# A table of planner settings replaced: 640 rows by 652, in a two-layer attention and feed-forward kernel on one core

## The chip, the cores and the metric

One NeuronCore of one Trainium2 chip runs the program. The metric is device time in microseconds (us) of one launch, as the median of several executions; lower is better. Five engines work side by side, each in its own fixed program order: PE (TensorE, matmuls), DVE (VectorE), ACT (ScalarE), POOL (GpSimd) and SP (which issues DMAs here).

## The reference

Two layers of attention and of a gated feed-forward block over 2048 tokens of width 512, with 32 heads of 16 channels. Both layers use the same weights.

```python
B, S, D, H = 1, 2048, 512, 32        # F = 1792
...
qkv = (x @ wqkv).reshape(B, S, 3, H, Dh)
scores = einsum("bhqd,bhkd->bhqk", q, k) * Dh ** -0.5
p = softmax(scores, axis=-1)
return einsum("bhqk,bhkd->bhqd", p, v).reshape(B, S, D) @ wo
...
return (gelu(x @ w_gate) * (x @ w_up)) @ w_down
...
x = x + attention(layernorm(x));  x = x + ffn(layernorm(x))
x = x + attention(layernorm(x));  x = x + ffn(layernorm(x))
```

## The kernel before

**Work.** Attention is cut into units: a block of up to 512 query tokens times a group of four heads. Each unit's scores are computed twice. The first pass (called p1 in the code) has queries on the partitions and 512 keys along a PSUM bank; it serves only to find the maximum of each row. The second pass (p2) has keys on the partitions and queries along the bank; there the exponential is taken, and its result goes as weights into the matmul with the values. A score matmul uses 32 of the 128 rows of the PE, so four of them for four heads can run beside each other.

**Which engine does what.**
- PE: first-pass scores at L2564, second-pass scores at L2442, probabilities times values at L2467 (four matmuls for each tile of 512), all projections and feed-forward matmuls at L1309, transposes at L1438, and filler matmuls on zeros at L2597, whose result nobody reads. The planner puts fillers in where it reckons that PE has been too idle in the last 3.4 us.
- DVE: the row maxima at L2579, over one bank (output 128x1) or two banks at once (128x2).
- ACT: the exponentials at L2414, over one bank (128x512) or two (128x1024), and copies out of PSUM.
- A folded tile: PE forms the difference of two key tiles' scores (L2387, from keys subtracted on POOL at L2144), ACT takes its positive part (L2394), and DVE adds it to the other tile's scores and takes the maximum in one custom instruction (L2574, followed by a read-out of its accumulator). So one DVE instruction covers two tiles.
- POOL: softmax sums, layer norm, the polynomial around the tanh of the gelu (L1856 to L1866), and the gate's product (L2066, L2084) after ACT has copied the up-projection out (L2064, L2082). The same product can be made by DVE alone (L2059, L2076).
- SP: moves of queries and keys into place and the transposes by DMA.

**What sets the order.** The host runs a planner before the launch: the loop at the end of `_build`. It keeps an estimated clock for each engine, and at each step it emits the next first-pass piece, the next second-pass piece, a value matmul, a piece of other work (a projection, a feed-forward matmul) or a filler. What it emits is appended to the engines' streams; on the chip each engine follows its stream strictly, with semaphores between engines. PSUM's eight banks are shared out: banks 0 to 3 take first-pass tiles, 4 to 6 second-pass tiles and other work, 7 the value sums. When the second pass lags behind, the planner can lend bank 3 and work on pairs there (`bmode`, `lend`), and DVE then gets more single banks.

Twenty numbers steer the choices: how long to wait for a pair (`SPC`, `SPLIT`), how far ahead of DVE and ACT to emit (`S1C`, `S2C`), how much other work may delay scores (`OV`, `LIM`), how far the second pass may lag (`LAG`, `LAGT`, `LAGX`), how many tiles to fold (`FL`, `GL`, `FX`), how large the pieces of other work are (`PIECE`, `GP`), and so on. They are taken from the table `PLAN` anew at each stretch, that is, for every 2 steps of first-pass position (a step is two tiles of 512):

```python
now = clk["pe"]
if pos["p1"] >= STRETCH * stretch[0]:
    if stretch[0] in PLAN:
        SPC, SPLIT, S1C, S2C, OV, LIM, NT, P2B, LAG, LAGT, FL, GL, FX, AHD, DUE, DUEM, PIECE, GP, NPV, LAGX = PLAN[stretch[0]]
    stretch[0] += 1
```

A row stays in force until the next one. There are 4096 tiles in each pass, so some 1024 stretches. What is computed is the same for any table; the order, the pairing and the folding differ.

Of the kernel before, what the change touches and what calls it, by code (L numbers as in the profile page):

```python
# [822 lines left out]
def _build(nc, x_in, wqkv, wo, wg, wu, wd, out, layer_blocks=((512, 512, 512, 512), (512, 512, 512, 256, 256)),  # L823
# [16 lines left out]
    with es:  # L840
# [62 lines left out]
        clk = {e: 0.0 for e in ("pe", "act", "dve", "pool", "sp", "dma")}  # L903
# [1924 lines left out]
```

## Time and profile before

| | us |
|---|---|
| median of 3 runs | 2442.04 |
| lowest and highest | 2441.47 and 2442.51 |
| the profiled execution's own time | 2441.87 |
| its span, first to last instruction | 2440.2 |
| PE busy in it | 2380.9 |
| DVE busy in it | 2382.1 |
| ACT busy in it | 2326.3 |
| POOL busy in it | 1351.0 |

The profile shows one execution. "Busy" is the time in which at least one instruction of the engine was running; instructions of one engine overlap at their ends, so a mean duration is longer than what one more instruction adds. A row of groups reads: line, engine, operation, output and input, shapes, count, then busy time and mean duration in nanoseconds, then the idle time just ahead of those instructions and who ended it.

### The profile page before, as it was taken

Reading aid. Unit: us, or ns where it says so; the run is one execution under the profiler, and the core shown is the slowest. Engines: PE = TensorE matmul, PEld = TensorE weight load, DVE = VectorE, ACT = ScalarE, POOL = GpSimd, SP = SyncE. Lnnn points to the kernel's source line nnn. Section 1 sums busy time; section 2 is a strip of 40 time slices with the busy share of each in tenths; the row PEclk is TensorE's granted clock in tenths of the full one; section 3 lists DMA queues with packets and bytes.
Section 4 is the critical chain, followed back from the end, with each engine's and each line's share of the span. In section 5 each row is a group of like instructions: output and inputs, shape, how many; then the busy total and the mean of one; then the engine's idle time right before and its main releaser. Section 6 shows DMA issues by size and latency. Waiting matters only on the chain.

```text
span 2440.2 us, 69860 instructions
## 1 busy us (share of the span) xinstructions
PE 2380.9 (98%) x29929; PEld 1149.2 (47%) x29929; DVE 2382.1 (98%) x3203; ACT 2326.3 (95%) x3275; POOL 1351.0 (55%) x2232
## 2 busy tenths in 40 slices
PE   8999999999999999999999999999999999999999
PEld 3444544444444444444533455554444444444456
DVE  8999999999999999999999999999999999999995
ACT  7999999999999999999976999999999999999997
POOL 5121137967579756977752211278716892278462
PEclk9999999999999999999999999999999999999999
DMA  3110000000000001001010000000000000000000
GB/s 96 49 60 8 4 13 13 2 4 13 15 11 2 6 9 20 3 8 24 17 25 14 4 5 4 11 15 2 5 13 17 8 2 9 15 12 5 13 10 13
DMA packets 69678, 35.25 MB, mean 14 GB/s; under 512 B 51576, under 2 KB 68344, under 8 KB 69368
## 3 DMA queue, kind: packets, MB, share of 16 engines
q1 hardware_dynamic: 69368, 30.80, 5.2%
q8 instruction: 234, 3.83, 0.6%
q14 instruction: 76, 0.62, 0.1%
HBM read 9.70 MB, written 2.10 MB: 5 GB/s over the span
## 4 chain that ended last, share of the span: by engine, by line
PE 44%; DVE 39%; ACT 16%; issue 1%; POOL 0%; DMA 0%; SPq 0%; ACTq 0%; POOLq 0%; DVEq 0%
DVE PM L2579 36%; PE PS L2564 15%; ACT SCR L2414 14%; PE PS L2467 11%; PE PS L1309 10%; PE PS L2442 4%; PE PS L2597 4%; DVE SCR L2574 2%; ACT SCR L1862 0%; PE PS L2387 0%; ACT AO L2082 0%; ACT SCR L2394 0%; ACT HT L1326 0%; ACT SG L1326 0%; DVE AO L2125 0%
## 5 line engine op out<-in xcount | busy, mean ns | idle before, releaser
L2579 DVE TENSOR_REDUCE PM<-PS 128x2 f32<-128x1024 f32 (+1 forms) x2551 | 2190.7, 924 | 24.3 <-PE PS L2564 7.4
L2414 ACT ACTIVATE SCR<-PS 128x1024 bf16<-128x1024 f32 (+1 forms) x2590 | 2021.9, 886 | 51.6 <-PE PS L2442 34.9
L2564 PE MATMUL PS<-KT,QT 32*128 32x512 bf16 x3899 | 1038.6, 384 | 36.4 <-DVE PM L2579 21.5
L2442 PE MATMUL PS<-QT,KT 32*128 32x512 bf16 (+2 forms) x5120 | 934.3, 340 | 2.2 <-ACT SCR L2414 1.0
L2467 PE MATMUL PS<-VP,SCR 128*128 128x51 bf16 (+1 forms) x16384 | 818.0, 187 | 9.1 <-ACT SCR L2414 5.8
L2467 PEld LDWEIGHTS PS<-VP,SCR 128*128 128x128 bf16 x16384 | 581.7, 96 | 500.5 <-issue 414.0
L2564 PEld LDWEIGHTS PS<-KT,QT 32*128 32x128 bf16 x3899 | 247.5, 91 | 505.5 <-DVE PM L2579 303.2
L2597 PE MATMUL PS<-WV,ZER 128*128 128x240 bf16 x1961 | 370.7, 265 | 0.1
L1710 POOL TENSOR_TENSOR RL<-ACCS,CM 128x16 f32<-128x16 f32 (+2 forms) x70 | 181.1, 2587 | 305.8 <-ACT ACCS L1704 305.5
L2442 PEld LDWEIGHTS PS<-QT,KT 32*128 32x128 bf16 x5120 | 242.1, 91 | 55.9 <-ACT SCR L2414 28.6
L1651 POOL TENSOR_TENSOR PM<-PM 128x32 f32<-128x32 f32 (+2 forms) x80 | 19.1, 239 | 351.4 <-DVE PM L2579 341.2
L2597 PEld LDWEIGHTS PS<-WV,ZER 128*128 128x128 bf16 x1961 | 149.3, 96 | 55.6 <-issue 50.6
L1309 PE MATMUL PS<-WD,HT 128*128 128x512 bf16 x448 | 138.9, 381 | 0.2 <-ACT AO L1728 0.2
L1309 PE MATMUL PS<-XNT,WU 128*128 128x512 bf16 (+2 forms) x616 | 138.6, 323 | 0.5 <-ACT SCR L2394 0.3
L1309 PE MATMUL PS<-XNT,WG 128*128 128x512 bf16 (+2 forms) x616 | 137.3, 323 | 0.3 <-DVE XNT L1324 0.3
L2084 POOL TENSOR_TENSOR HT<-HT,AO 128x512 bf16<-128x512 bf16 (+1 forms) x96 | 104.3, 1089 | 45.0 <-ACT AO L2082 43.8
L2574 DVE CUSTOM_DVE_ANT_0 SCR<-PS,SCR 128x512 bf16<-128x512 f32 x197 | 126.1, 684 | 0.6 <-PE PS L2564 0.2
L2144 POOL TENSOR_TENSOR KD<-KT 128x512 bf16<-128x512 bf16 x78 | 89.9, 1152 | 65.9 <-PE PS L2387 60.6
L1856 POOL TENSOR_TENSOR SCR<-HT 128x512 bf16<-128x512 bf16 x98 | 101.8, 1039 | 31.2 <-ACT HT L1326 29.9
L2394 ACT ACTIVATE SCR<-PS 128x1024 bf16<-128x1024 f32 x99 | 104.5, 1056 | 13.7 <-PE PS L2387 8.9
L1866 POOL TENSOR_TENSOR HT<-HT,SCR 128x512 bf16<-128x512 bf16 x98 | 112.8, 1152 | 4.4
L1860 POOL TENSOR_TENSOR SCR<-SCR,HT 128x512 bf16<-128x512 bf16 x98 | 112.7, 1152 | 1.6
(130 smaller groups left out, 1493.5 us busy)
## 6 DMA issues: line engine op xcount, KB each, us to landing
KT<-SG SPq DMA_DIRECT2D x64, 64.0 KB
QT<-SG SPq DMA_DIRECT2D x52, 64.0 KB
QT<-MT SPq DMA_DIRECT2D x200, 1.0 KB
out_dram<-AO SPq DMA_DIRECT2D x16, 128.0 KB, 1.7
WG<-in_B_w_gate_dram SPq DMA_DIRECT2D x4, 448.0 KB, 4.8
WU<-in_B_w_up_dram SPq DMA_DIRECT2D x4, 448.0 KB, 5.2
QT<-MT SPq DMA_DIRECT2D x104, 0.5 KB
WD<-in_B_w_down_dram SPq DMA_DIRECT2D x4, 384.0 KB, 3.9
```

Source lines behind the costliest of these rows:

```text
L1309: ins = e.matmul(out_ap, lhsT=l, rhs=r_, start=(i == 0), stop=(i == n - 1))
L1710: emit("pool", lambda e: e.tensor_tensor(RL[:, s, 0:4 * nq], lsum, CM1[:, 0:4 * nq], op=ALU.pow), r=[("ACCS", s), ("CM1",)], w=[("RL", s)] ...
L1860: emit("pool", lambda e: e.tensor_tensor(u, u, ht, op=ALU.mult), r=ku + kh, w=ku, dur=0.18 + n / 520.0)
L1866: emit("pool", lambda e: e.tensor_tensor(ht, ht, u, op=ALU.mult), r=ku + kh, w=kh, dur=0.18 + n / 520.0)
L2394: emit("act", lambda e: e.activation(PT[:, s0:s0 + cnt, :], PS[:, bk:bk + cnt, :], ACTF.Relu), r=bks, w=[("PT", s0 + d) for d in range(cnt ...
L2414: emit("act", lambda e: e.activation(dst, src, ACTF.Exp, scale=DH ** -0.5), r=[BK[bk + i] for i in range(cnt)], w=[("PT", i) for i in slot ...
L2442: ins = e.matmul(bank(bk)[:, i * n:(i + 1) * n], lhsT=KT[32 * j:32 * j + 32, g, kt * 128:(kt + 1) * 128], rhs=QT[32 * j:32 * j + 32, s, c0 ...
L2467: ins = e.matmul(acc, lhsT=PT[:, slot, i * nh + (qt - q0) * 128:i * nh + (qt - q0 + 1) * 128], rhs=AP(VP, (kt * H + 4 * g + j) * 17, [[NTT ...
L2564: ins = e.matmul(bank(b), lhsT=QT[32 * j:32 * j + 32, s, qt * 128:(qt + 1) * 128], rhs=KT[32 * j:32 * j + 32, g, kb * 512:(kb + 1) * 512], ...
L2574: emit("dve", lambda e, i=i, b=b, sl=sl: e.tensor_tensor_reduce(PT[:, sl, :], bank(b), PT[:, sl, :], 1.0, -3.0e38, ALU.add, ALU.max, po[:, ...
L2579: emit("dve", lambda e: e.tensor_reduce(po, PS[:, bs[0]:bs[0] + cnt, :], axis=AX.X, op=ALU.max), r=bks, w=[("PM", sm) + h[1:] for h in hs] ...
L2597: return e.matmul(PS[:, b, NACC:512], lhsT=ZER[:, :], rhs=WV[:, 0, 0:512 - NACC], start=(b != 7), stop=(b != 7), skip_group_check=True)
```

## The change

`PLAN` is replaced: 652 rows in place of 640, and only 14 of them are as they were. The planner gets two further options, `PB` (when POOL is due, the planner gives it the most urgent chain) and `SLF` (layer norm on another path); both have the default 0, and nothing sets them, so the branches are not entered. The rest of the kernel is as it was; lines below the table stand 12 to 19 lines lower.

```diff
 PLAN = {
-    0: (0.3, 0.25, 0.55, 0.42, 0.0, -0.05, 1, 1, 62, 92, 8, 20, 0.5, 1.5, -10, 18, 1, 3, 7, 92),
-    1: (0.3, 0.05, 0.55, 0.42, 0.0, -0.05, 1, 1, 62, 0, 8, 20, 0.5, 1.5, -10, 18, 1, 3, 7, 92),
+    0: (0.3, 0.25, 0.55, 0.42, 0.0, -0.05, 1, 1, 62, 92, 8, 20, 0.5, 1.5, -5, 18, 1, 3, 7, 8),
+    1: (0.3, 0.25, 0.8, 0.42, 0.0, 0.0, 1, 1, 62, 92, 3, 80, 0.5, 1.5, -5, 18, 2, 1, 7, 30),
...
-           ... XDN=2, PK=1, LT=0, RCD=0):
+           ... XDN=2, PK=1, LT=0, RCD=0, PB=0, SLF=0):
...
-            ln = ln_fast if fast else ln_pool if LNP and ...
+            ln = ln_fast if fast or (SLF and LT and tts[0] >= SLF and ((tag[0] == "mid") == (tag[1] == 0))) else ln_pool if LNP and ...
...
-                            if est(a[1], a[2]) > now + 0.3:
+                            if (PB and a[0] == "pool") or est(a[1], a[2]) > now + 0.3:
                                 break
...
+                if PB and clk["pool"] <= now + PB + 1e-6:
+                    ready = [c for c in chains if not c.done and c.ann[0] == "pool" and est(c.ann[1], c.ann[2]) <= now + 0.3]
+                    if ready:
+                        min(ready, key=lambda c: c.due).step()
+                        changed = True
...
+                    if PB and a[0] == "pool":
+                        nxt.append(clk["pool"] - PB)
```

The new table moves nearly every instruction of every engine, but the counts change little. Counted over the whole streams (lines as before the change):

| engine, instruction | before | changed |
|---|---|---|
| DVE L2579 maximum over one bank | 1400 | 1392 |
| DVE L2579 maximum over two banks | 1151 | 1152 |
| DVE L2574 folded tile | 197 | 200 |
| DVE L1324 copy to SG, 512 wide | 5 | 6 |
| DVE L2059 gate product, 512 wide | 5 | 2 |
| DVE L2076 gate product, 512 wide | 2 | 3 |
| ACT L2414 exponential over two banks | 1506 | 1459 |
| ACT L2414 exponential over one bank | 1084 | 1178 |
| ACT L2394 positive part, two banks / one | 98 / 1 | 99 / 2 |
| ACT L2082 / L2064 copy, 512 wide | 82 / 9 | 81 / 12 |
| ACT L1326 copy to SG, 512 wide | 51 | 50 |
| PE L2564 first-pass score tiles | 3899 | 3896 |
| PE L2597 fillers | 1961 | 1866 |
| PE changes between score matmuls (32 rows) and full matmuls (128 rows) | 5374 | 5426 |

Of the exponentials of the first 2048 second-pass tiles (the first layer), 544 were over one bank and 752 over two; now 642 and 703. In the second layer it was 541 and 754, now 537 and 756.

The first place is ACT in the first layer, from the copy-out that ends the 26th unit (L1704, now L1716). L2414 is the exponential, L1326 and L2082 are copies out of PSUM, L1862 a tanh. Before:

```order
L1704 ACTIVATE ACCS<-PS 128x272
L2414 ACTIVATE SCR<-PS 128x512
L1326 ACTIVATE SG<-PS 128x256
L2414 ACTIVATE SCR<-PS 128x1024
L2414 ACTIVATE SCR<-PS 128x512
L2414 ACTIVATE SCR<-PS 128x1024
L2414 ACTIVATE SCR<-PS 128x512
L1326 ACTIVATE HT<-PS 128x512
L2414 ACTIVATE SCR<-PS 128x1024
```

The same place on ACT in the changed kernel:

```order
L1716 ACTIVATE ACCS<-PS 128x272
L2426 ACTIVATE SCR<-PS 128x512 x3
L1338 ACTIVATE HT<-PS 128x512
L2426 ACTIVATE SCR<-PS 128x512 x7
L1874 ACTIVATE SCR<-SCR 128x512
L2426 ACTIVATE SCR<-PS 128x512 x2
L1338 ACTIVATE HT<-PS 128x512
L2426 ACTIVATE SCR<-PS 128x512 x5
```

Exponentials that stood in turn over two banks and over one now come over one bank each: the unit that follows has 60 single and 2 double ones, where it had 22 and 21.

The second place is the end of the first pass on PE. L2564 (now L2576) is the last first-pass score tile; L2442 are second-pass scores, eight matmuls of 128 columns for two tiles, L2467 value matmuls, L1309 with WD the feed-forward's down projection. Before:

```order
L2564 MATMUL PS<-KT,QT 128x512
L2467 MATMUL PS<-VP,SCR 128x3x17 x4
L1309 MATMUL PS<-WD,HT 128x512 x2
L2442 MATMUL PS<-QT,KT 128x128 x16
L2467 MATMUL PS<-VP,SCR 128x51 x4
L2467 MATMUL PS<-VP,SCR 128x3x17 x4
L1309 MATMUL PS<-WD,HT 128x512 x5
L2442 MATMUL PS<-QT,KT 128x128 x8
```

The same place on PE in the changed kernel:

```order
L2576 MATMUL PS<-KT,QT 128x512
L2454 MATMUL PS<-QT,KT 128x128 x8
L2479 MATMUL PS<-VP,SCR 128x3x17 x12
L2479 MATMUL PS<-VP,SCR 128x51 x4
L2454 MATMUL PS<-QT,KT 128x128 x8
L1321 MATMUL PS<-WD,HT 128x512 x2
L2454 MATMUL PS<-QT,KT 128x128 x8
```

From there to the end the streams are nearly alike. Behind the last first-pass tile stand 160 second-pass matmuls of 128 columns (40 tiles) where there were 168 (42 tiles), and 45 down-projection matmuls where there were 51.

More of the change, by code (lines that the diff above doesn't have):

```diff
@@ L823, in _build @@
 def _build(nc, x_in, wqkv, wo, wg, wu, wd, out, layer_blocks=((512, 512, 512, 512), (512, 512, 512, 256, 256)),
-           n_ahead=6, n_pre=6, S1C=0.45, S2C=0.42, OV=0.3, PD=80, FDUE=20, LIM=-0.05, NT=1, AHD=2.0, DUEM=2, FDL2=0, OPD=12, URG=0.3, ft_tok=512, n_pt=8, n_qt=8, SPLIT=0.15, SPC=0.1, PVC=47, WARM=0.55, WARML=0.42, NPV=7, BOOST=0.0, LAG=62, LAGT=84, GP=2, SING=0, DUE=0, END=360, LAGE=10, FD=205, FDL=-10, QD=60, KD_=16, VD=20, FL=8, FMAX=6, NKD=2, FLOOK=2, FX=0.3, GF=0, FAST=1, TG=1, GS=2, P2B=1, PIECE=2, GL=60, GLE=20, HARD=-1e9, LNP=1, LNPT=12, PREO=1, SPL=2, OPL=1, BM=1, LAGB=60, PREO0=1, LNPT0=8, LNPT1=8, QH0=2, QH1=2, OPS=12, FDS=0, FD3=205, FDA=0, SPL0=4, VCH=0, TA=0, TC=0, X3=0, TH=0, HQ=0, TP=1, LAGX=84, G2=0, CAL=0, XD=15, XDT=0.6, XDN=2, PK=1, LT=0, RCD=0):
+           n_ahead=6, n_pre=6, S1C=0.45, S2C=0.42, OV=0.3, PD=80, FDUE=20, LIM=-0.05, NT=1, AHD=2.0, DUEM=2, FDL2=0, OPD=12, URG=0.3, ft_tok=512, n_pt=8, n_qt=8, SPLIT=0.15, SPC=0.1, PVC=47, WARM=0.55, WARML=0.42, NPV=7, BOOST=0.0, LAG=62, LAGT=84, GP=2, SING=0, DUE=0, END=360, LAGE=10, FD=205, FDL=-10, QD=60, KD_=16, VD=20, FL=8, FMAX=6, NKD=2, FLOOK=2, FX=0.3, GF=0, FAST=1, TG=1, GS=2, P2B=1, PIECE=2, GL=60, GLE=20, HARD=-1e9, LNP=1, LNPT=12, PREO=1, SPL=2, OPL=1, BM=1, LAGB=60, PREO0=1, LNPT0=8, LNPT1=8, QH0=2, QH1=2, OPS=12, FDS=0, FD3=205, FDA=0, SPL0=4, VCH=0, TA=0, TC=0, X3=0, TH=0, HQ=0, TP=1, LAGX=84, G2=0, CAL=0, XD=15, XDT=0.6, XDN=2, PK=1, LT=0, RCD=0, PB=0, SLF=0):
     S = x_in.shape[1]
@@ L1467, in ln_to_xnt @@
         def ln_to_xnt(tts, tag, ready, due, fast=False):
-            ln = ln_fast if fast else ln_pool if LNP and tts[-1] < (LNPT if tag[0] == "in" else (LNPT0, LNPT1)[tag[1]]) else ln_head
+            ln = ln_fast if fast or (SLF and LT and tts[0] >= SLF and ((tag[0] == "mid") == (tag[1] == 0))) else ln_pool if LNP and tts[-1] < (LNPT if tag[0] == "in" else (LNPT0, LNPT1)[tag[1]]) else ln_head
             if LT:
```

1260 rows, old and new, of the table PLAN are left out of this document.

## The prediction

> **What bounds the kernel now.** I read the page first, for busy shares and the granted clock:
>
> ```profile
> span 2440.2 us, 69860 instructions
> PE 2380.9 (98%) x29929; PEld 1149.2 (47%) x29929; DVE 2382.1 (98%) x3203; ACT 2326.3 (95%) x3275; POOL 1351.0 (55%) x2232
> ...
> DVE  8999999999999999999999999999999999999995
> ACT  7999999999999999999976999999999999999997
> ...
> PEclk9999999999999999999999999999999999999999
> ...
> PE 44%; DVE 39%; ACT 16%; issue 1%; POOL 0%; DMA 0%; SPq 0%; ACTq 0%; POOLq 0%; DVEq 0%
> ...
> L2579 DVE TENSOR_REDUCE PM<-PS 128x2 f32<-128x1024 f32 (+1 forms) x2551 | 2190.7, 924 | 24.3 <-PE PS L2564 7.4
> ```
>
> Three engines are nearly full, and the chain of waits passes among PE, DVE and ACT. DVE is idle least. Its row maxima alone (L2579) take 2190.7 us. The view by windows, cut at the layer crossing and the tail, shows where DVE is not full (the third figure behind the length is DVE, the fourth ACT):
>
> ```profile
> core 0: us, PE busy (x) PEld busy (x) DVE busy (x) ACT busy (x) POOL busy (x), PEclk, DMA share, GB/s
> 0.00:61.00 61.00, 54.74 (x362) 24.23 (x363) 54.61 (x115) 45.65 (x68) 35.79 (x72) 0.97 0.32 96
> 61.00:671.00 610.00, 594.95 (x7595) 287.81 (x7594) 607.59 (x827) 602.78 (x788) 288.30 (x519) 1.00 0.07 18
> 671.00:1220.00 549.00, 540.04 (x6743) 253.23 (x6744) 545.50 (x687) 537.25 (x800) 411.91 (x665) 1.00 0.06 11
> 1220.00:1342.00 122.00, 117.25 (x868) 47.39 (x867) 119.00 (x221) 82.54 (x119) 48.27 (x113) 1.00 0.09 20
> 1342.00:1830.00 488.00, 479.27 (x6415) 237.62 (x6415) 481.35 (x611) 481.97 (x593) 201.78 (x305) 1.00 0.03 7
> 1830.00:2379.00 549.00, 536.82 (x7024) 259.66 (x7021) 541.13 (x674) 532.14 (x832) 351.13 (x532) 1.00 0.04 10
> 2379.00:2440.00 61.00, 57.79 (x935) 39.22 (x933) 32.97 (x74) 44.02 (x81) 13.87 (x28) 1.00 0.05 13
> ```
>
> From 61 to 2379 us DVE is idle for 2.41 + 3.50 + 3.00 + 6.65 + 7.87 = 23.4 us of 2318. So the time is: DVE's work up to the last row maximum, its idle time on the way, and a tail behind it. The waits of DVE say who makes the idle time:
>
> ```profile
> DVE AO L2125 <- PE PS L1309: 15.3, 4, 8.8
> DVE PM L2579 <- PE PS L2564: 7.4, 18, 1.2
> DVE PM L2579 <- PE PS L2442: 7.2, 33, 0.6
> ```
>
> L2125 belongs to the tail. In the body DVE waits for PE, 14.6 us, because PE has other work queued ahead of the next score tile. The rest of the idle time are gaps too short to be listed.
>
> **The change part by part.** The settings compute nothing; they decide order, pairing, folding and filling. So I cost the counts first, then what order alone can do.
>
> *DVE's work.* The groups by shape:
>
> ```profile
> L2414 ACT ACTIVATE SCR<-PS 128x1024 bf16<-128x1024 f32 x1506 | 1457.0, 1076 | 37.2 <-PE PS L2442 25.8 <-DVE PM L2574 0.4 <-PE PS L2564 0.2
> L2579 DVE TENSOR_REDUCE PM<-PS 128x2 f32<-128x1024 f32 x1151 | 1398.4, 1218 | 17.0 <-PE PS L2442 5.1 <-PE PS L2564 5.0 <-PE PS L2387 0.3
> L2579 DVE TENSOR_REDUCE PM<-PS 128x1 f32<-128x512 f32 x1400 | 938.8, 682 | 7.3 <-PE PS L2564 2.4 <-PE PS L2442 2.1
> L2414 ACT ACTIVATE SCR<-PS 128x512 bf16<-128x512 f32 x1084 | 616.1, 622 | 14.4 <-PE PS L2442 9.0
> L2574 DVE CUSTOM_DVE_ANT_0 SCR<-PS,SCR 128x512 bf16<-128x512 f32 x197 | 126.1, 684 | 0.6 <-PE PS L2564 0.2 <-PE PS L2442 0.2
> L2574 DVE DVE_READ_ACCUMULATOR2_ANT PM<- 128x1 f32 x197 | 16.4, 83 | 0.0
> L2059 DVE TENSOR_TENSOR HT<-PS,HT 128x512 bf16<-128x512 f32 x5 | 3.4, 684 | 0.0
> ```
>
> Neighbours overlap, so the means (1218 and 682 ns) are too long for what one more costs. A second bank adds 1218 - 682 = 536 ns. With the page's 2190.7 us for all 2551, a single one adds (2190.7 - 1151 x 0.536) / 2551 = 0.617 us and a double one 1.153. The changed streams have 8 singles fewer, -4.9 us, and 1 double more, +1.2. Three folded tiles more cost 3 x (0.64 + 0.08) = +2.2 at most (126.1 / 197, and the read-out 16.4 / 197). One copy more to SG is +0.6 (512 wide from PSUM, as L2059, less the same 65 ns of overlap), three L2059 fewer -1.9, one L2076 more +0.6. Sum: **-2.2 us**.
>
> The three gate products that leave DVE go to ACT (L2064) and POOL (L2066). POOL is busy for 55% and hides them; without that cover each would cost ACT about one single exponential.
>
> *ACT's work.* 47 double exponentials become 94 single ones; the first layer alone gives up 49, the second gains 2. At the means, one split costs 2 x 622 - 1076 = 168 ns, together +7.9 us. At what one more adds (2021.9 us for all 2590 from the page's L2414 row below, second bank 454 ns, so 0.517 and 0.971) it is 63 ns, together +2.9 us.
>
> ```profile
> L2414 ACT ACTIVATE SCR<-PS 128x1024 bf16<-128x1024 f32 (+1 forms) x2590 | 2021.9, 886 | 51.6 <-PE PS L2442 34.9
> ...
> 1403.00:1647.00 244.00, 239.65 (x3363) 124.31 (x3360) 241.23 (x304) 243.98 (x272) 81.05 (x154) 1.00 0.04 9
> 61.00:1220.00 1159.00, 1134.99 (x14337) 541.04 (x14336) 1153.09 (x1513) 1140.03 (x1587) 700.20 (x1184) 1.00 0.06 15
> ```
>
> From 61 to 1220 us, the first layer's attention, ACT is idle for 1159 - 1140.03 = 19.0 us, DVE for 5.9. I cost the splits at **0**, hidden behind DVE; if that cover is gone they cost 3 to 8 us (a rival below). Only in the second layer, 1403 to 1647 us, does ACT stand still for just 0.02 us. That is a run of double exponentials with which the second pass catches up, 358 in a row; the changed stream has 361, and it begins 32 first-pass tiles earlier and covers 540 in place of 539. Three doubles more are 2.9 us there and 2.9 us fewer elsewhere. I count it as moved, 0.
>
> *The tail.* After the last row maximum ACT runs on through double exponentials nearly without a gap, then PE does the last gate, up and down projections:
>
> ```profile
> 2391.96 5.43 DVE L2579 TENSOR_REDUCE PM<-PS 128x2 f32<-128x1024 f32 x6
> ...
> 2397.32 6.52 ACT L2414 ACTIVATE SCR<-PS 128x1024 bf16<-128x1024 f32 x7 [0.64 <-PE PS L2442]
> 2403.72 0.24 ACT L1704 ACTIVATE ACCS<-PS 128x68 f32<-128x68 f32 x1
> 2403.83 7.58 ACT L2414 ACTIVATE SCR<-PS 128x1024 bf16<-128x1024 f32 x8
> ```
>
> The last maximum ends at 2391.96 + 5.43 = 2397.4, so the tail is 42.8 us. Two tiles fewer stand in it, one double exponential: 6.52 / 7 = 0.93, so **-0.9 us**. The six down-projection matmuls fewer lie between exponentials, beside ACT, and count 0. Everything from the last exponential on is the same instruction for instruction.
>
> *DVE's idle time on the way.* Three pieces of the chain in the tail give prices for PE's work:
>
> ```profile
> 2402.71 0.31 PE PS L2467 x8
> 2404.67 0.62 PE PS L2467 x20
> 2415.10 0.41 PE PS L2597 x4
> ```
>
> The idle time is what order alone can change, and no row gives it, so I bound it. If all of the body ran as the first part does (2.41 us idle in 610, 0.395%), 2318 us would hold 9.2 us, a gain of 14.3. If all ran as the last part does (7.87 in 549, 1.43%), it would hold 33.2, a loss of 9.8. Two counts say which end is nearer. One is PE's fillers, put in where the planner found PE waiting: 95 fewer, at 0.41 / 4 = 0.10 us each, -9.7 us. Against that stand 52 more changes between score and full matmuls, 26 more runs. A run of value matmuls costs (0.62 - 0.31) / 12 = 0.026 us for each and 0.31 - 8 x 0.026 = 0.10 once, so +2.7 us. PE is asked for 7.0 us less in all. The other count is of places where more than 1.1 us of other PE work (at such prices) stands between two first-pass steps: about 95 before, about 90 now; at 14.6 us for all, -0.8 us. Between -0.8 and -7.0 I take **-3.0 us**, on the side of the first part.
>
> A rule of the Trainium skill speaks against leaving fillers out: "TensorE: Matmul & The Clock Gate", Part 1, says that after an idle window of about 3.4 us the PE clock falls to half. Before the change the trace shows 1.00 in every window behind 61 us, so no run here shows that rule at work in the body. By the rule the sum would be that of the last rival.
>
> **Sum.** -2.2 - 0.9 - 3.0 = -6.1 us, with splits, moved catch-up and POOL at 0. The profiled execution took 2441.87 us (1.67 more than its span, which I keep). It lies 0.17 under the median of 2442.04. So 2441.87 - 6.1 = **2435.8 us**.
>
> **The rivals.**
>
> *Only moved.* The counts hold, but DVE's idle time stays as it is: what one stretch gains another gives back. For it speaks that DVE's work is the same to 0.1%, and that 14.6 us of listed waits are spread over 51 places. Against it, the 95 fillers. Time 2441.87 - 2.2 - 0.9 = 2438.8.
>
> *ACT becomes the bound in the first layer (the other side).* Each engine keeps its order, so where ACT is late PE stands before the next second-pass matmul, and DVE behind it. Place: units such as the one shown, with 60 single exponentials and 2 double ones where it had 22 and 21. Price: 49 splits in the first layer at 168 ns, 8.2 us, with nothing hidden. It decides from the point where ACT's idle time there, 19.0 us in 1159, isn't at the units with the singles. For it speaks that DVE keeps only 5.9 us of its own idle time there to absorb a late PE. Against it, that ACT has three times as much as DVE. Time 2441.87 - 2.2 - 0.9 + 8.2 = 2447.0, slower.
>
> *A clock lapse.* Fewer fillers let the granted clock fall. In the first window the clock reads 0.97, some 61 x 0.03 = 1.8 us lost; four such lapses in the body would cost 7.3 us against the forecast: 2443.1, and more would pass the old time by over 0.2%. Against it, a clock of 1.00 in every later row, and fillers still 1866.
>
> That the change doesn't do what it says I give no chance: the streams differ everywhere, and the two new options are off.
>
> **How the numbers follow.** A measurement of this kernel can tell about 0.2%, 4.9 us, from no change: 2437.2 and 2446.9 are the marks. Forecast 0.48 (2435.8, its own range 2428 to 2437), only moved 0.34 (within), ACT 0.13 (slower), clock 0.05 (0.02 within, 0.03 slower). So faster 0.48, same 0.36, slower 0.16. The full gain of idle time would give 2441.87 - 3.1 - 14.3 = 2424.5 and the full loss 2448.6. The range leaves a tenth out at each end: 2428 to 2446.
>
> **What would show it.** DVE busy about 2380 us, with 1392 single and 1152 double maxima at 682 and 1218 ns. DVE idle from 61 us to 61 us before the end about 20 us in place of 23.4; under 16 or over 30 says that order did more than I gave it. A tail of about 42 us behind the last maximum. ACT over the first layer with idle time left, some 12 to 16 us in place of 19.0; if it stands at under 5, ACT was the bound. A granted clock of 1.00 in every window. The prediction is wrong if DVE's waits for PE grow, above all in the first layer, where they were smallest.

## The result, and the profile after

| | before | changed | difference |
|---|---|---|---|
| median of 7 runs each, us | 2441.68 | 2433.83 | -7.85 |
| lowest and highest, us | 2441.26 to 2442.51 | 2433.37 to 2434.70 | |
| span of the profiled execution, us | 2440.2 | 2432.1 | -8.1 |
| ratio of the times | | 0.9968 | 95% interval 0.9957 to 0.9980 |

The changed kernel is faster, by a little more than the 6.1 us forecast, and inside the range. The page of the changed kernel, in the order in which the prediction read the old one:

```profile
span 2432.1 us, 69441 instructions
PE 2339.3 (96%) x29581; PEld 1144.6 (47%) x29834; DVE 2375.5 (98%) x3201; ACT 2326.5 (96%) x3325; POOL 1356.5 (56%) x2236
...
PEclk9999999999999999999999999999999999999999
...
DVE 36%; ACT 31%; PE 29%; POOL 2%; issue 1%; DMA 0%; SPq 0%; POOLq 0%; ACTq 0%; DVEq 0%
...
L2591 DVE TENSOR_REDUCE PM<-PS 128x1 f32<-128x512 f32 (+1 forms) x2544 | 2184.3, 923 | 24.3 <-PE PS L2454 8.8
```

PE's figure is not to be compared: 29581 matmuls stand against 29834 weight loads, so some 250 matmul records are missing from this trace. So the drop of 41.6 us in PE's busy time, and its fall in the chain from 44% to 29%, can't be read as a gain: part of them is the 95 fillers fewer, part missing records. DVE is busy for 6.6 us less, nearly all of it in the row maxima (2190.7 to 2184.3). ACT is busy for as long as before, although it has 47 exponentials more.

The view by windows, with the columns of the prediction's table (length; PE, PEld, DVE, ACT, POOL; clock):

```profile
61.00:671.00 610.00, 587.09 (x7520) 287.15 (x7565) 607.10 (x830) 603.67 (x803) 290.34 (x525) 1.00 0.07 18
671.00:1220.00 549.00, 529.91 (x6685) 255.04 (x6757) 545.04 (x697) 539.37 (x835) 412.11 (x663) 1.00 0.06 11
1220.00:1342.00 122.00, 116.48 (x863) 46.67 (x867) 120.03 (x219) 82.36 (x117) 47.66 (x111) 1.00 0.09 20
1342.00:1830.00 488.00, 472.28 (x6386) 236.56 (x6427) 480.75 (x605) 485.05 (x621) 203.89 (x306) 1.00 0.03 7
1830.00:2371.00 541.00, 522.77 (x6862) 254.81 (x6926) 533.88 (x666) 525.60 (x805) 354.13 (x534) 1.00 0.05 10
```

DVE's idle time from 61 us to 61 us before the end is 2.90 + 3.96 + 1.97 + 7.25 + 7.12 = 23.2 us; it was 23.4. By the view of waits the two listed waits of the maxima for PE sum to 14.3 us; they were 14.6:

```profile
DVE PM L2591 <- PE PS L2454: 8.8, 38, 0.7
DVE PM L2591 <- PE PS L2576: 5.5, 13, 1.2
```

So 8 us went, and the idle time on which the prediction put 3 of them is where it was. Most of the 8 went from time that the profile calls busy. Behind a maximum over one bank the next maximum begins 598 ns after that one's start, and behind one over two banks 1132 ns; these are the medians of the start-to-start times in both traces, taken here as the spacing where nothing is waited for. Yet the groups by shape give longer means of one:

```profile
L2591 DVE TENSOR_REDUCE PM<-PS 128x2 f32<-128x1024 f32 x1152 | 1397.2, 1216 | 17.0 <-PE PS L2454 6.1 <-PE PS L2576 4.2 <-PE PS L2399 0.3
L2591 DVE TENSOR_REDUCE PM<-PS 128x1 f32<-128x512 f32 x1392 | 930.6, 680 | 7.3 <-PE PS L2454 2.7 <-PE PS L2576 1.3
```

680 - 598 and 1216 - 1132 are some 82 to 84 ns. An instruction that begins up to that much late still begins before the last one has ended. It loses time, and the engine never shows as idle. Among pairs of neighbouring maxima, the mean spacing behind one over a single bank was 638 ns before and is 635 now; behind one over two banks it is 1137 in both. The late ones are the single banks, and they are a little less late.

With those spacings the time up to the last maximum can be split into work (each maximum at its median spacing, a folded tile at 607 + 60 ns, any other instruction at its duration less 85 ns) and lateness (all the rest, idle or not). Each stage ends with the DVE instruction that completes a given number of the 4096 first-pass tiles (256, 2048, 2560, 3584, 4096), the same in both kernels. The last column says how much sooner the changed kernel gets there:

```
first-pass tiles      work before  now      diff   lateness before  now   diff   end of stage
first 1/16 (fill)       148.5     148.4     -0.1        9.0         8.1   -0.9       -1.0
2nd to 8th             1000.0     999.8     -0.2       15.5        15.8   +0.3       -0.9
9th, 10th (crossing)    270.8     270.8      0.0        6.7         4.7   -2.1       -3.0
11th to 14th            607.6     606.3     -1.3       20.7        18.5   -2.1       -6.4
15th, 16th              306.9     305.9     -1.0       10.7        11.7   +1.0       -6.4
```

Over all (from the unrounded figures) the work fell by 2.5 us and the lateness by 3.8. The first layer (the first eight sixteenths) gave nothing beyond its fill, and the last two sixteenths gave nothing either; the gain is made at the crossing of the layers and in the 11th to 14th sixteenth. Behind the last maximum stands the tail. First DVE's last run of maxima, then ACT, by the timeline of the changed kernel (start, length, what, count; a row that joins several shapes names one, and the nine exponentials at 2387.97 are two over one bank and seven over two):

```profile
2385.62 5.41 DVE L2591 TENSOR_REDUCE PM<-PS 128x2 f32<-128x1024 f32 x6 [0.23 <-PE PS L2454]
...
2387.97 7.82 ACT L2426 ACTIVATE SCR<-PS 128x512 bf16<-128x512 f32 x9
2395.67 0.23 ACT L1716 ACTIVATE ACCS<-PS 128x68 f32<-128x68 f32 x1
2395.78 7.58 ACT L2426 ACTIVATE SCR<-PS 128x1024 bf16<-128x1024 f32 x8
...
2403.35 5.62 ACT L2426 ACTIVATE SCR<-PS 128x1024 bf16<-128x1024 f32 x6
```

The last maximum ends at 2385.62 + 5.41 = 2391.0, where it was 2397.4: -6.4. From there to the end it is 41.1 us, where it was 42.8: -1.7. From the copy-out at 2395.67 (before: 2403.72) to the end the two agree, at 36.4 us. So the tail's gain lies between the last maximum and that copy, 4.6 us where it was 6.3: seven exponentials over two banks began there before, five begin there now (from 2391.08 us on, some 0.92 apart).

**At the crossing** one can see what became less late. ACT's timeline before, in the first unit of the second layer:

```profile
1333.74 1.94 ACT L2414 ACTIVATE SCR<-PS 128x1024 bf16<-128x1024 f32 x2 [0.56 <-PE PS L2442]
1336.24 2.00 ACT L2414 ACTIVATE SCR<-PS 128x1024 bf16<-128x1024 f32 x3 [0.56 <-PE PS L2442]
1338.56 3.87 ACT L2414 ACTIVATE SCR<-PS 128x1024 bf16<-128x1024 f32 x5 [0.32 <-PE PS L2442]
...
1357.95 0.39 ACT L1704 ACTIVATE ACCS<-PS 128x272 f32<-128x272 f32 x1
```

And after:

```profile
1323.99 29.77 ACT L2426 ACTIVATE SCR<-PS 128x1024 bf16<-128x1024 f32 x32 [1.03 <-PE PS L2454]
1353.58 0.47 ACT L1716 ACTIVATE ACCS<-PS 128x272 f32<-128x272 f32 x1
```

Before, the exponentials of this unit come in runs of one to seven, with waits of some 0.2 to 0.6 us for second-pass scores between them; now 32 run without a gap. ACT's waits from 1320 to 1360 us (in total, times, longest), before and then after, of which the longest is each time the one ahead of the unit's first exponential:

```profile
ACT SCR L2414 <- PE PS L2442: 11.6, 14, 6.2
```

```profile
ACT SCR L2426 <- PE PS L2454: 6.3, 2, 5.3
```

From 1320 to 1360 us ACT is busy for 17.96 + 16.02 = 33.98 us before and 19.82 + 18.00 = 37.82 us now, by the view of windows, before and then after:

```profile
1320.00:1342.00 22.00, 21.53 (x299) 11.01 (x295) 21.65 (x31) 17.96 (x21) 2.98 (x12) 1.00 0.02 3
1342.00:1360.00 18.00, 17.26 (x252) 8.83 (x251) 17.54 (x27) 16.02 (x18) 4.73 (x14) 1.00 0.01 3
```

```profile
1320.00:1342.00 22.00, 21.14 (x318) 10.88 (x316) 21.80 (x31) 19.82 (x22) 3.28 (x14) 1.00 0.02 3
1342.00:1360.00 18.00, 17.41 (x273) 9.38 (x272) 17.71 (x26) 18.00 (x21) 6.53 (x14) 1.00 0.01 2
```

The copies of the value sums out of PSUM (L1704, now L1716) mark the same place of the program in both, and show how the second pass gains a lead, if not steadily: -1.4 us at the last unit of the first layer (1222.27 to 1220.88), -4.4 at the first unit of the second (1357.95 to 1353.58), between -1.3 and -6.6 from there to 2086 us, -6.3 at the unit that ended at 2134.73, and -8.1 at the end.

### The profile page after: what moved, and what is told of

It reads as the page before. It is cut to its first block, busy times and chain, and to the rows that moved or that the text cites. A ratio compares the mean times of both kernels' runs of the same rounds, so it can differ in the third digit from the quotient of the medians.

```text
span 2432.1 us, 69441 instructions
## 1 busy us (share of the span) xinstructions
PE 2339.3 (96%) x29581; PEld 1144.6 (47%) x29834; DVE 2375.5 (98%) x3201; ACT 2326.5 (96%) x3325; POOL 1356.5 (56%) x2236
## 4 chain that ended last, share of the span: by engine, by line
DVE 36%; ACT 31%; PE 29%; POOL 2%; issue 1%; DMA 0%; SPq 0%; POOLq 0%; ACTq 0%; DVEq 0%
DVE PM L2591 33%; ACT SCR L2426 28%; PE PS L2576 10%; PE PS L1321 8%; PE PS L2479 6%; PE PS L2454 3%; PE PS L2609 2%; DVE SCR L2586 2%; ACT SCR L2406 1%; ACT SCR L1874 1%; PE PS L2399 0%; ACT HT L1338 0%; ACT AO L2094 0%; POOL HT L1878 0%; ACT ACCS L1716 0%
## 5 line engine op out<-in xcount | busy, mean ns | idle before, releaser
L2591 DVE TENSOR_REDUCE PM<-PS 128x1 f32<-128x512 f32 (+1 forms) x2544 | 2184.3, 923 | 24.3 <-PE PS L2454 8.8
L2426 ACT ACTIVATE SCR<-PS 128x512 bf16<-128x512 f32 (+1 forms) x2637 | 2020.4, 878 | 39.2 <-PE PS L2454 24.8
L2576 PE MATMUL PS<-KT,QT 32*128 32x512 bf16 x3896 | 1039.3, 384 | 50.7 <-DVE PM L2591 24.6
L2576 PEld LDWEIGHTS PS<-KT,QT 32*128 32x128 bf16 x3896 | 247.5, 91 | 500.2 <-DVE PM L2591 307.0
L2609 PE MATMUL PS<-WV,ZER 128*128 128x240 bf16 x1866 | 350.9, 265 | 1.1 <-ACT SCR L2426 0.5
L2609 PEld LDWEIGHTS PS<-WV,ZER 128*128 128x128 bf16 x1866 | 141.9, 96 | 47.0 <-issue 40.7
L1321 PE MATMUL PS<-XNT,WG 128*128 128x512 bf16 (+2 forms) x562 | 121.1, 317 | 5.3 <-issue 3.2
L1321 PE MATMUL PS<-XNT,WU 128*128 128x512 bf16 (+2 forms) x552 | 121.6, 316 | 3.8 <-issue 2.9
L1321 PE MATMUL PS<-WD,HT 128*128 128x512 bf16 x380 | 119.3, 381 | 4.2 <-issue 2.4
L2406 ACT ACTIVATE SCR<-PS 128x1024 bf16<-128x1024 f32 (+1 forms) x101 | 105.8, 1049 | 15.5 <-PE PS L2399 11.3
```

What stands on the lines that cost most here:

```text
L1321: ins = e.matmul(out_ap, lhsT=l, rhs=r_, start=(i == 0), stop=(i == n - 1))
L2406: emit("act", lambda e: e.activation(PT[:, s0:s0 + cnt, :], PS[:, bk:bk + cnt, :], ACTF.Relu), r=bks, w=[("PT", s0 + d) for d in range(cnt ...
L2426: emit("act", lambda e: e.activation(dst, src, ACTF.Exp, scale=DH ** -0.5), r=[BK[bk + i] for i in range(cnt)], w=[("PT", i) for i in slot ...
L2576: ins = e.matmul(bank(b), lhsT=QT[32 * j:32 * j + 32, s, qt * 128:(qt + 1) * 128], rhs=KT[32 * j:32 * j + 32, g, kb * 512:(kb + 1) * 512], ...
L2591: emit("dve", lambda e: e.tensor_reduce(po, PS[:, bs[0]:bs[0] + cnt, :], axis=AX.X, op=ALU.max), r=bks, w=[("PM", sm) + h[1:] for h in hs] ...
L2609: return e.matmul(PS[:, b, NACC:512], lhsT=ZER[:, :], rhs=WV[:, 0, 0:512 - NACC], start=(b != 7), stop=(b != 7), skip_group_check=True)
```

## The experiments

All are timed against the kernel before, side by side on the same chip. "Share" means: us measured, divided by the us that were added to one engine at the prices of the prediction. It is given with the interval that follows from the ratio's.

**Which half of the table does it.** Rows below 512 steer the first layer's first pass, rows from 512 on the second's. First the new rows below 512 with the old ones behind:

```diff
 PLAN = {
-    0: ... 511: (rows before)
+    0: ... 511: (rows of the change)
     512: ... (rows before)
```

> The kernel before, with the new table's rows up to stretch 511 (the first layer's share) and its own old rows from 512 on. If the two halves of a table are worth something by themselves, this takes the first half's part of the change: the first-pass position of the layer crossing came at 1190.0 us before and 1190.7 us after, so +0.7 us, ratio 1.000. If the rows only fit the state that they were chosen in, the old rows meet another state here and do worse: this stream has 1470 single and 1124 double maxima and 189 folded tiles, which at 0.617, 1.153 and 0.72 us is +6.3 us of DVE work against before, ratio about 1.003 or more.

Measured: 2486.46 us, ratio 1.0181 (1.0167 to 1.0195), 45 us slower than before. (The 1190.0 and 1190.7 us of the expectation are where half of the tiles outside folds are done, which is not the same tile in both; the 2048th tile was done at 1174.0 us before and 1173.1 after the change.) Then the other way round, the old rows below 512 and the new ones from there:

```diff
 PLAN = {
     0: ... 511: (rows before)
-    512: ... (rows before)
+    512: ... (rows of the change)
```

> The kernel before, with its own old rows up to stretch 511 and the new table's rows from 512 on. If the halves are worth something by themselves, this holds nearly the whole gain, since the two traces stand level at the crossing and differ by 8 us at the end: about -8 us, ratio 0.9965. If rows only fit their own state, the stream's counts decide: 1414 single and 1152 double maxima, 189 folded tiles, +4.0 us of DVE work, ratio about 1.002 or more.

Measured: 2487.32 us, ratio 1.0184 (1.0169 to 1.0200). Each half worsens when the other is exchanged, so the gain can't be divided between them. The windows of the two mixtures, first the one with the new first half, show where it begins to go wrong:

```profile
1220.00:1342.00 122.00, 116.83 (x775) 45.41 (x785) 116.98 (x217) 74.64 (x117) 48.32 (x109) 1.00 0.10 24
1342.00:1830.00 488.00, 474.98 (x6177) 236.40 (x6213) 475.79 (x615) 469.51 (x591) 202.23 (x300) 1.00 0.03 6
```

```profile
1220.00:1342.00 122.00, 116.06 (x752) 45.91 (x759) 117.27 (x210) 71.81 (x108) 46.48 (x99) 1.00 0.10 22
1342.00:1830.00 488.00, 471.14 (x6273) 236.13 (x6315) 469.05 (x596) 478.09 (x607) 204.92 (x312) 1.00 0.03 7
```

DVE is idle for 5.0 and 4.7 us in the crossing, where the matched tables leave 3.0 and 2.0, and for 12.2 and 19.0 us behind it, where they leave 6.7 and 7.3. By the split into work and lateness, the traced run of the first mixture has 11.6 us more work than before, 27 more lateness (24 of it from the crossing to the 14th sixteenth) and a tail longer by 6.0; the second, by a trace that took 2.5 us more than its median, has 2.0, 33 and 12.6. So the loss is mostly lateness and not a matter of counts. In both mixtures the rows fit badly to a state that other rows left.

**Does a row of the wrong state carry anything at all?** The changed kernel with its own rows below 512 and its row 0 from there on, and then with row 0 alone:

```diff
 PLAN = {
     0: ... 511: (rows of the change)
-    512: ... (rows of the change)
+    512: (row 0 of the change)
```

> The changed kernel with its own rows up to stretch 511 and one row for all the rest, row 0 of its table: settings that were never chosen for the second layer. The old rows put there (1.0181 of before) cost some 44 us against before and 52 against the changed kernel. If a row chosen in another state still carries something of the second layer's needs, one row for all of it does clearly worse than that, ratio 1.025 or more. If it carries nothing, the two are alike, ratio 1.018 within 0.3%.

```diff
 PLAN = {
     0: (row 0 of the change)
-    1: ... (all other rows)
```

> The changed kernel with row 0 of its table as the only row, in force for the whole program. If the choice of rows is worth as much in the first layer as in the second, the loss against the changed kernel is about twice that of one row for the second layer alone. If the second layer alone depends on it, the two are alike. Counted: 1350 single and 1295 double maxima and 78 folded tiles, so by counts alone (0.617, 1.153, 0.72 us) 51 us more DVE work than before.

Measured: 2507.61 us, ratio 1.0266 (1.0248 to 1.0285), and 2549.18, ratio 1.0432 (1.0414 to 1.0451). Foreign rows for the second layer (1.0181) beat this single row there (1.0266), so they still carry something; no other single row was tried. Row 0 for the second layer costs 73.8 us against the changed kernel (2507.61 less 2433.83), and row 0 in the first layer too costs another 41.6. So the choice of rows counts in both layers, and less in the first. Against some 115 us between one row and all 652 (2549.18 less 2433.83), the 7.85 from the old table to the new are a small step.

**What DVE's work is worth.** The term of -2.2 us took DVE's time at its full price. Here maxima over two banks are issued as two over one, with the planner's clocks moved on as for one, so that the order stays as it is. First every 11th, 104 in all:

```diff
+ if cnt == 2 and n_max[0] % 11 == 0:
+     for i, b in enumerate(bs):
+         sch.op("dve", lambda e, i=i, b=b: e.tensor_reduce(po[:, i:i + 1], bank(b), axis=AX.X, op=ALU.max), ...)
+     clk["dve"] = start + 0.066 + cnt * 0.5317
```

> The kernel before, with every 11th maximum over two banks (104 of 1151) issued as two over one bank each, 208 singles more; the planner reckons as if nothing had changed, so the order on PE and ACT is the same. If DVE's work sets the body and one more instruction costs what the groups give (2 x 0.617 - 1.153 = 0.081 us), it takes 104 x 0.081 = +8.4 us, ratio 1.0034. If PE or ACT set the pace, DVE's 23 us of idle time take it in: 0 to +2 us.

Measured: 2443.92 us, ratio 1.0010 (1.0001 to 1.0019), +2.0 us. One split adds 2 x 0.617 - 1.153 = 0.081 us, 104 of them 8.4: a share of 0.24 (0.03 to 0.55). By the split into work and lateness the trace has 6.4 us more work and 4.4 less lateness. Then every 4th, 287 in all (% 4 in the same place):

> The kernel before with every 4th double maximum issued as two single ones (287 of 1151). 104 such splits cost +2.0 us in place of 8.4. If DVE has some 60 us of slack and takes more work in at a steady share, 287 cost 287 / 104 x 2.0 = +5.7 us. If the slack is used up place by place, the share rises: between 5.7 and 287 x 0.081 = +23.2 us.

Measured: 2448.63 us, ratio 1.0026 (1.0016 to 1.0036), +6.2 of 23.2 us: a share of 0.26 (0.17 to 0.38). The share is no higher at the larger load, though DVE is then the larger part of the chain of waits (39% before):

```profile
DVE 52%; PE 36%; ACT 10%; POOL 1%; issue 1%; POOLq 0%; ACTq 0%; DVEq 0%
```

The share has a second reading. In these kernels each of the two maxima waits for its own bank alone and releases it when it is done, where the maximum over two waits for both and holds both. So these shares are what a split costs, with that help in it, and not surely what DVE's time alone costs; the runs don't part the two. The same holds for the exponentials below. The base matters too: at the median spacings a split adds 2 x 598 - 1132 = 64 ns and not 81, and both shares become about a third.

**What a split exponential costs.** Every 8th exponential over two banks in the first layer is issued as two, 94 in all, the order kept in the same way:

```diff
+ if cnt == 2 and units[u][0] == 0 and n_exp[0] % 8 == 0:
+     for i in range(2):
+         sch.op("act", lambda e, i=i: e.activation(PT[:, slots[i], :], bank(bk + i), ACTF.Exp, scale=DH ** -0.5), ...)
+     clk["act"] = start + sw + 0.055 + cnt * 0.4267
```

> The kernel before, with every 8th double exponential of the first layer (94 of 752) issued as two single ones; the planner reckons as if nothing had changed. The change has 49 such splits in the first layer, so this is about twice its dose. If ACT's idle time there (19 us in 1159) hides them: within 1.5 us of before, ratio 1.000. If ACT is the bound at those places: 94 x 0.063 = +5.9 us at what one more adds, up to 94 x 0.168 = +15.8 us at the means, ratio 1.0024 to 1.0065.

Measured: 2444.77 us, ratio 1.0012 (1.0003 to 1.0021), +2.9 of 94 x 0.063 = 5.9 us: a share of 0.49 (0.12 to 0.87). Not hidden, then, though ACT has 19.0 us of idle time there. The same for every third of units 37 to 46, 106 in all, in the run where ACT never stands still:

```diff
+ if cnt == 2 and 37 <= u <= 46 and n_exp[0] % 3 == 0:
```

> The kernel before with every 3rd double exponential of the units 37 to 46 issued as two single ones (106 splits; the second layer's run of doubles, in which ACT stood still for 0.02 us of 244). If ACT is the bound there, as that row says: 106 x 0.063 = +6.7 us at what one more adds, up to +17.8 us at the means. If the pace there is DVE's or PE's: like the 94 splits of the first layer, about +3 us.

Measured: 2447.75 us, ratio 1.0026 (1.0017 to 1.0035), +5.3 of 6.7 us: a share of 0.79 (0.62 to 1.28). By its window ACT is busy for all of 244 us, and DVE has 5.1 us of idle time where it had 2.8:

```profile
1403.00:1647.00 244.00, 240.87 (x3303) 124.18 (x3300) 238.87 (x298) 244.00 (x352) 81.32 (x154) 1.00 0.04 8
```

This fits ACT as the bound there, or nearly; the interval doesn't rule out less.

**Are 95 fillers fewer a cause?** They were the reason for the size of the idle-time term. The kernel before without every 20th filler, 98 of 1961, with the planner reckoning them as if they were there:

```diff
+ n_fill[0] += 1
+ if n_fill[0] % 20 == 0:
+     sch.op = lambda *a, **k: None
  ... (the filler matmul)
+ sch.__dict__.pop("op", None)
```

> The kernel before, with every 20th filler matmul left out (98 of 1961; they compute nothing that is read), all else in the same order. If fillers hold up score matmuls, 98 fewer are worth up to 98 x 0.10 = -9.8 us, and the change's gain would be theirs. If fillers only stand where PE waits anyway, as my stall term took most of them to do, 0 to -2 us, ratio 0.999 to 1.000.

Measured: 2442.48 beside 2442.09 us, ratio 1.0006 (0.9997 to 1.0015): no gain. The interval leaves room for 0.7 us of gain at most (the lowest runs differ by as much, 2440.78 beside 2441.45), where 98 at 0.10 us are 9.8. So nearly all of these 98 stand where PE waits anyway. They are spread evenly; that the 95 of the change are alike wasn't tried. Then the opposite, 96 extra filler matmuls right ahead of first-pass score tiles, one for every 28 steps:

```diff
+ n_p1[0] += 1
+ if n_p1[0] % 28 == 0:
+     n_p1[1] += 1
+ if n_p1[1] and est(w=[BK[7]]) <= clk["pe"] - 0.1:
+     sch.op("pe", lambda e: e.matmul(PS[:, 7, NACC:512], lhsT=ZER[:, :], ...))
```

> The kernel before with 96 more filler matmuls, each put straight ahead of a first-pass score tile (every 28th step), where PE has work to do; the planner doesn't know of them, so the rest of the order is the same. If PE sets the pace of the body, each costs its 0.10 us, and 0.10 more where it breaks up a run of score matmuls: +9.6 to +19 us, ratio 1.004 to 1.008. If DVE sets it, as my sum took it, PE's delay is taken in by the banks ahead of DVE: 0 to +3 us.

Measured: 2445.48 us, ratio 1.0015 (1.0006 to 1.0024), +3.0 of 9.6 us: a share of 0.31 (0.15 to 0.61). So the same matmul costs next to nothing where the planner put it and counts for about a third of its length ahead of a score tile.

**What the fillers are for.** The changed kernel without its 1866 fillers (they multiply zeros, and nothing else is left out), the planner reckoning them as if they were there:

```diff
+ if True:
+     sch.op = lambda *a, **k: None
```

> The changed kernel without any filler matmul (1866 left out; they compute nothing that is read), all else in the same order. If fillers are what keeps PE's clock at full rate, the granted clock falls well under 1.00 and the time rises, by tens of us or more. If the clock stays without them, PE is asked for 187 us less (1866 x 0.10) and DVE's waits for PE shrink: the clock at 1.00 and a time some 0 to 20 us under the changed kernel's.

Measured: 2656.07 us, ratio 1.0863 (1.0826 to 1.0901). Its page, and its window from 61 to 671 us:

```profile
PE 2535.3 (95%) x27716; PEld 1154.1 (43%) x27968; DVE 2420.3 (91%) x3201; ACT 2394.4 (90%) x3325; POOL 1356.6 (51%) x2236
...
PEclk8855556898559976998898655579886688689889
```

```profile
61.00:671.00 610.00, 582.71 (x6138) 256.55 (x6184) 556.46 (x750) 558.11 (x724) 257.20 (x462) 0.70 0.06 16
```

The granted clock falls to 0.70 in that window and 0.77 over the run. So the fillers hold the clock up, and 95 fewer were still enough: the changed kernel's clock is 1.00 in every window shown above.

## Why the prediction was right, and where its steps were not

**Direction and size** held: -6.1 us forecast, -7.85 measured. As an account of where the time went, the sum held too: -2.5 of DVE's work (-2.2 forecast), -3.8 of lateness (-3.0, forecast as idle time) and -1.7 of tail (-0.9) make -8.0, which is the span's change but for rounding. What the single steps were worth as causes is another matter.

**DVE's work, -2.2.** By the split of DVE's time it fell by 2.5, so the prices and the counts were right. What the runs speak against is the step from work to time, "-2.2" taken at full price: splits that added DVE work cost 0.24 and 0.26 of its length (0.03 to 0.55 and 0.17 to 0.38), and in the first of them lateness shrank by 4.4 us of the 6.4 added. Taken the other way, which no run did, 2.2 us less work are worth about 0.6.

**ACT's splits, 0.** "Hidden behind DVE" doesn't stand: the 94 splits of the first layer were not hidden. At their share of 0.49 (0.12 to 0.87) the 49 splits of the first layer, 49 x 0.063 = 3.1 us, cost about 1.5. ACT's idle time there did shrink as foretold, from 19.0 to 1159 - 603.67 - 539.37 = 16.0 us (12 to 16 were forecast); but 19 us of idle time in 1159 aren't a cover for every place. The rival in which ACT becomes the bound of the first layer fell: it asked for +8.2, and the first layer ended 1.4 us earlier. In the very unit that it named, with 60 single exponentials and 2 double ones, the time from copy to copy went from 39.2 to 39.9 us; in another, with 55 and 4 where there were 21 and 22, it went from 39.2 down to 37.4.

**The catch-up run, 0.** ACT stands still for 0.13 us of the 244 from 1403 to 1647 us, as before (0.02). The run was moved, not relieved: it now lasts from 1321.0 to 1659.7 us, where it lasted from 1340.5 to 1679.1.

**The tail, -0.9.** The mechanism held, its size was off: -1.7. Counted was one double exponential fewer, from PE's order behind its last first-pass tile; two are gone, seven to five, since ACT also has one more of them done by the time of the last maximum. 2 x 0.92 is 1.8.

**DVE's idle time, -3.0.** This is the step that was read wrongly. The idle time stayed at 23.2 against 23.4 (about 20 was forecast), and the waits for PE at 14.3 against 14.6 (some 2 of either lie in the first 61 us, which the prediction's "body" leaves out). The prediction named a growth of these waits in the first layer as a sign of being wrong: from 61 to 1220 us the two waits listed above went from 1.7 to 2.6 us, and DVE's idle time from 5.9 to 6.9. It is small, and the crossing and what follows made up for it, but it is the opposite of what the term asked for. The lateness fell by 3.8 all the same, inside what counts as busy. Nor is the reason for its size borne out as a cause: taking 98 other fillers out gained 0.7 us at most.

**What order alone was worth.** With the shares as prices, the span's -8.1 us less the tail (-1.7), less DVE's work (-0.6), less the splits (+1.5) leaves about -7.3 for the order alone, where the prediction took -3.0 between bounds of -14.3 and +9.8. That is worked out, not measured: the shares have wide intervals, come from work added to the kernel before, and the change removes some. By this reckoning two errors stood against each other, on the one side a full price for DVE's work and none for ACT's splits, on the other too little for the order, and that the sum came out better than its terms is luck.

**The other rivals.** "Only moved" (2438.8) asked for unchanged idle time, and got it, but not its time: the gain doesn't show as idle time. The clock lapse didn't come; the clock is 1.00 behind 61 us.

**What is shown and what isn't.** Shown by the traces: at the crossing ACT's short waits for second-pass scores went and DVE's lateness fell by 2.1 us; in the 11th to 14th sixteenth the lateness fell by another 2.1 and DVE's work by 1.3; the tail is shorter by 1.7. Shown by the runs: each half of the new table, put together with the other half of the old one, is 1.8% slower than the old table and 2.2% slower than the new one. Not shown: that ACT's smoother run at the crossing is what made DVE less late there. Not isolated: which rows make the lateness fall behind the crossing, since a mixture of rows changes all that follows it, by 45 us here.

## What to carry to other kernels

Where three engines pass the chain of waits between them, one us of work more on one of them need not be one us more of time: here it was 0.24 to 0.26 on DVE, 0.31 on PE and 0.49 on ACT (0.79 where ACT never rests), each with a wide interval, and a few splits with the order kept give such a price. Read spacing from start to start rather than busy and idle time, since an instruction that begins too late to overlap its neighbour, but before it ends, costs time that the views of busy and idle time don't list. Compare stages at the same tile: a cut that is off by three tiles moves some 1.7 us from one stage to the next, as much as the effects looked for here. A table of settings that was chosen step by step belongs to its own history: compare whole tables, since half of a good one is worse than either.

## What the runs showed of the hardware that was not expected

Without fillers the granted clock fell to 0.77 although the page still shows PE busy for 95% of the span; busy time so read doesn't tell whether the clock is held. The Trainium skill, "TensorE: Matmul & The Clock Gate", Part 1, says that the clock falls to half after an idle window of about 3.4 us. The run agrees that it falls to half, but not that it takes an idle time of that length: from 160 to 400 us the clock is 0.50 with PE busy for 234 of the 240 us, and PE's longest idle time in the whole trace is 2.2 us. With the fillers in, every slice reads 0.9 or more. How many are enough wasn't tried between 0 and 1866.

ACT's busy time in a group can fall with more instructions, since neighbours overlap: ACT has 47 exponentials more in the changed kernel, and the group's busy time went from 2021.9 to 2020.4 us:

```profile
L2426 ACT ACTIVATE SCR<-PS 128x512 bf16<-128x512 f32 (+1 forms) x2637 | 2020.4, 878 | 39.2 <-PE PS L2454 24.8
```
